# A small input loaded as 16 rows of 36 elements and spread by four accumulating matmuls, in place of 64 rows of nine and one

## The chip, the cores and the metric

One core of a Trainium2 chip. The metric is the device time of one execution, in microseconds (us). Every run here counts as fast unless it lies over 1.5% above the fastest of its kernel.

## The reference

Two attention layers with one query each, side by side. A looks at the last 2,048 of 8,192 cached keys and values (W = min(4096, max(256, 8192/4))), B at all of them. Cut to what matters:

```python
D, Hq, Hkv, Sk, Dh = 576, 32, 16, 8192, 128        # x: [1, 1, 576], bf16
q = (x @ wq).reshape(B, Sq, Hq, Dh)                # wq: [576, 4096]
scores = einsum(q, k) * Dh ** -0.5                 # two query heads per cached head
o = softmax(scores) @ v
out = o.reshape(B, Sq, Hq * Dh) @ wo               # wo: [4096, 576]; A and B concatenated
```

x has 1,152 bytes for each layer. The caches that are read and the weights have 102.76 MB.

## The kernel before

A helper records every operation with what it reads and writes, and works out the waits. The engines are SP (issues the large loads), ACT, DVE, POOL and PE. For the projection the kernel wants, in each of 128 partitions, nine values of x: partition p holds part p // 2, and odd and even partitions use different halves of them. x is loaded as 64 rows of nine, and a matmul with a matrix `twice`, an identity with each column doubled, copies row p // 2 to partition p:

```python
    xnine = nc.alloc_sbuf_tensor("xnine", [64, 2, 9], BF16)
    twice = nc.alloc_sbuf_tensor("twice", [64, 128], BF16)
    # ... cut
    def load_x(P):                                     # issued from ACT, P = 0 for A, 1 for B
        def go(act):
            return act.dma_start(xnine[:, P, :], xs[P][0, 0, :].rearrange("(m r) -> m r", m=64))
        add("act", go, writes=[("xnine", P)], dma="x%d" % P)
    # ... cut: POOL clears tiles, then makes the identity
    add("dve", lambda dve: dve.tensor_copy(twice[:, :].rearrange("p (m e) -> p m e", e=2), <identity, each column twice>),
        reads=["ident"], writes=["twice"])
    add("pe", lambda pe: pe.matmul(misc[:, 320:338], lhsT=twice[:, :], rhs=xnine[:, :, :].rearrange("p a r -> p (a r)"),
                                   start=True, stop=True),
        reads=[("xnine", 0), ("xnine", 1), "twice"], writes=[B_M])
```

What follows, in order:

```python
    WQ = [(4 * SLOT - WQ_W, [("v", 2)]), (SLOT, [("k", 1, 0), ("k", 1, 1), ("v", 0)])]
    for P in range(2):
        off, res = WQ[P]
        x_columns(P)                       # DVE: four masked copies of the spread x
        load(slots[:, off:off + WQ_W], <wq of P>, res, "wq%d" % P)      # SP, 4,608 KB
        q_part(P, off, res)                # PE: 36 matmuls of 512 columns, the projection
        q_finish(P)                        # ACT copy, PE turns, DVE copy
    # ... cut
    for g in range(NG):                    # group 0 is A, groups 1 to 4 are B
        for s in range(2):
            load_k(g, s)                   # SP; s = 1 reuses the place of wq of B
        load_v(g)                          # SP; reuses the place of wq of A
        # ... cut: transposes, scores, softmax, weighted sum
```

All large loads are issued from SP in one order. And the second half of K of A (`load_k(0, 1)`) is put where wq of B lies, so SP waits for the second projection before it issues that load, and every load behind it waits too.

## Time and profile before

| | before |
|---|---|
| time, median of 3 runs | 245.37 us (245.37 to 245.59) |
| profiled span | 244.0 us |
| bytes read | 102.76 MB, 421 GB/s over the span |
| PE, ACT, DVE, POOL busy | 68%, 38%, 36%, 3% |
| x of B lands | 17.8 us |
| first, second projection start | 18.82, 24.80 us |
| second half of K of A is issued | 28.24 us |

How to read it: the lines are shown in the prediction below. In a timeline the columns are start, duration, engine, source line, operation, tiles, count, and in brackets how long the engine had idled and what ended it. "PEld" is the load of a matmul's weights, "SPq" the queue of loads issued from SP. An engine's idle time matters only if it stands on the chain that ends last; here the row of the transfer engines, busy in all slices but the last, is the first thing to look at. A group of instructions is cut at the edge of the window that was asked for: the line of the first projection in the prediction (x32, 3.60 us) ends at 22 us; whole, it is x36 and 4.03 us. The trace also has a record of every DMA packet: its start, length and bytes. Figures said to come from the packet records are from there.

### The profile page before, as it was taken

What the parts mean: (1) busy time and instruction counts of PE and PEld (TensorE: products, weight loads), DVE (VectorE), ACT (ScalarE), POOL (GpSimd) and SP (SyncE); (2) the same over time, 40 slices, a digit from 0 to 9 for tenths busy, and PEclk for the clock granted to TensorE, in tenths of its full rate; (3) what the DMA queues carried; (4) which work ended last, traced back from release to release, by engine and by line L of the source; (5) the groups of instructions that cost most, each with busy time, mean ns of one, the idle gap of its engine ahead of it and who ended that gap; (6) DMA issues with size and microseconds to landing.
All of it is one profiled execution on the core that took longest, in us unless ns stands there. A gap on an engine that the chain in (4) does not pass through costs nothing. (4 is left out here: it accounts for less than half of the span.)

```text
span 244.0 us, 5212 instructions
## 1 busy us (share of the span) xinstructions
PE 165.8 (68%) x2325; PEld 120.5 (49%) x2325; DVE 88.2 (36%) x152; ACT 93.2 (38%) x96; POOL 6.4 (3%) x33
## 2 busy tenths in 40 slices
PE   0007539958397997394999473999446699845964
PEld 0002238745237775243978231987332687535753
DVE  0001218855304555203465322456322165533030
ACT  2000018845303876301687500678600387630000
POOL 5000100000000000000000000000000000000000
PEclk9999959997867999657699959799958799965799
DMA  9999999999999999899999999999989999989994
GB/s 344 429 405 422 435 432 422 427 424 427 459 432 426 489 397 462 371 430 435 483 410 451 403 403 435 435 494 408 473 365 440 430 494 397 473 380 417 426 405 172
DMA packets 4064, 102.88 MB, mean 422 GB/s; under 512 B 596, under 2 KB 728, under 8 KB 984
## 3 DMA queue, kind: packets, MB, share of 16 engines
q1 hardware_dynamic: 3896, 102.76, 98.3%
q8 instruction: 6, 0.10, 0.2%
q10 hardware_dynamic: 160, 0.00, 0.0%
q14 instruction: 2, 0.02, 0.0%
HBM read 102.76 MB, written 0.00 MB: 421 GB/s over the span
## 5 line engine op out<-in xcount | busy, mean ns | idle before, releaser
L506 ACT ACTIVATE kt<-ktps 128x1024 bf16<-128x1024 bf16 x80 | 79.8, 1040 | 87.3 <-PE ktps L496 87.2
L496 PE MATMUL ktps<-ident,slots 128*128 128x128 bf16 x1280 | 87.9, 234 | 22.6 <-PEq L214 19.6
L496 PEld LDWEIGHTS ktps<-ident,slots 128*128 128x128 bf16 x1280 | 81.7, 106 | 38.5 <-issue 38.5
L509 DVE COPY kt<-ktps 128x1024 bf16<-128x1024 bf16 x80 | 60.7, 774 | 59.6 <-PE ktps L496 59.6
L588 PE MATMUL opsum<-slots,ptm 128*32 128x512 bf16 x320 | 27.4, 515 | 7.7 <-PEq L214 7.7
L521 PE MATMUL sacc<-kt,qst 128*32 128x512 bf16 x320 | 25.8, 398 | 2.3 <-PEq L214 2.3
L588 PEld LDWEIGHTS opsum<-slots,ptm 128*32 128x32 bf16 x320 | 13.3, 125 | 20.3 <-issue 18.0
L559 PE MATMUL misc<-ident,psb 128*128 128x128 bf16 x40 | 4.3, 271 | 15.8 <-PEq L214 15.8
L547 ACT ACTIVATE psb<-sacc,stat 128x2048 bf16<-128x2048 f32 x5 | 9.8, 1967 | 9.8 <-DVE stat L536 9.8
L606 DVE TENSOR_TENSOR vtmp<-opsum,maskV 128x512 f32<-128x512 f32 x4 | 2.8, 691 | 27.7 <-PE opsum L588 27.7
L438 PE MATMUL misc<-xnine,twice 64*128 64x18 bf16 x1 | 0.2, 170 | 17.8 <-DMA xnine<-in_B_x_dram 17.8
L559 PEld LDWEIGHTS misc<-ident,psb 128*128 128x128 bf16 x40 | 3.1, 118 | 18.3 <-issue 18.3
L521 PEld LDWEIGHTS sacc<-kt,qst 128*32 128x32 bf16 x320 | 5.0, 94 | 8.4 <-issue 4.9
L566 DVE TENSOR_TENSOR ptm<-misc,maskP 128x1024 bf16<-128x1024 bf16 x5 | 3.5, 692 | 15.6 <-PE misc L559 15.6
L438 PEld LDWEIGHTS misc<-xnine,twice 64*128 64x128 bf16 x1 | 0.1, 99 | 17.8 <-issue 17.8
L703 ACT ACTIVATE outsb<-ktps 64x144 bf16<-64x144 f32 x1 | 0.3, 288 | 21.1 <-PE ktps L691 21.1
L691 PE MATMUL ktps<-slots,opj 128*32 128x144 bf16 (+1 forms) x192 | 6.8, 247 | 2.2 <-DMA slots<-in_B_wo_dram 2.2
L462 ACT ACTIVATE qrow<-opsum 128x512 bf16<-128x512 f32 x1 | 0.6, 597 | 19.2 <-PE opsum L456 19.2
L691 PEld LDWEIGHTS ktps<-slots,opj 128*32 128x32 bf16 x192 | 5.2, 97 | 3.6 <-DMA slots<-in_B_wo_dram 3.0
L447 DVE TENSOR_SCALAR xpad<-misc,par 128x5 bf16<-128x5 f32 (+1 forms) x8 | 1.2, 228 | 13.6 <-PE misc L438 13.6
L481 POOL COPY qst<-qcol 128x32 bf16<-128x32 bf16 x8 | 1.7, 213 | 147.5 <-PE sacc L521 147.5
L559 PE MATMUL turned<-ident,psb 128*128 128x128 bf16 x40 | 5.3, 314 | 0.0
(76 smaller groups left out, 57.9 us busy)
## 6 DMA issues: line engine op xcount, KB each, us to landing
slots<-in_B_k_cache_dram SPq DMA_DIRECT2D x8, 4096.0 KB
slots<-in_A_k_cache_dram SPq DMA_DIRECT2D x4, 2048.0 KB
slots<-in_A_v_cache_dram SPq DMA_DIRECT2D x4, 2048.0 KB
slots<-in_A_wq_dram SPq DMA_DIRECT2D x1, 4608.0 KB, 13.9
slots<-in_B_wq_dram SPq DMA_DIRECT2D x1, 4608.0 KB, 24.0
slots<-in_A_wo_dram SPq DMA_DIRECT2D x1, 4608.0 KB, 19.8
slots<-in_B_wo_dram SPq DMA_DIRECT2D x1, 3024.0 KB, 26.6
slots<-in_B_wo_dram SPq DMA_DIRECT2D x1, 1008.0 KB, 9.2
```

The costliest lines, as they stand in the source:

```text
L447: add("dve", lambda dve, dst=dst, o=320 + 9 * P + i, n=n, e=e: dve.tensor_scalar(dst, misc[:, o:o + n], par2[:, e:e + 1], None, ALU.mult), ...
L481: return pool.tensor_copy(dst, src)
L496: ins = pe.matmul(ktps_bf[q][:, t * 128:(t + 1) * 128], lhsT=slots[:, o:o + 128], rhs=ident[:, :], start=True, stop=True, is_transpose=True)
L506: add("act", lambda act, src=src, dst=dst: act.activation(dst, src, ACT.Copy), reads=[("bank", q)], writes=[("kt", u % NKT, q)], tag="e%d% ...
L509: add("dve", lambda dve, src=src, dst=dst: dve.tensor_copy(dst, src), reads=[("bank", q)], writes=[("kt", u % NKT, q)], tag="e%d%d" % (u, q))
L521: ins = pe.matmul(sacc[32 * j:32 * j + 32, :], lhsT=qst[:, o:o + 32], rhs=rhs, start=(u == 0 and e == 0), stop=True, skip_group_check=True)
L547: return act.activation(dst, src, ACT.Exp, bias=st(C_NB + g), scale=SCALE, accum_out=st(C_L + g))
L559: ins = pe.matmul(dst[:, t * 128:(t + 1) * 128], lhsT=psb[:, o:o + 128], rhs=ident[:, :], start=True, stop=True, is_transpose=True)
L566: return dve.tensor_tensor(ptm[:, c * 1024:(c + 1) * 1024].rearrange("p (t y) -> p t y", t=8), dst.rearrange("p (t y) -> p t y", t=8), mas ...
L588: ins = pe.matmul(opsum[64 * j + 32 * x:64 * j + 32 * x + 32, :], lhsT=ptm[:, o:o + 32], rhs=v[:, at[0], at[1], :, :, b:b + 128], start=(n ...
L606: add("dve", lambda dve: dve.tensor_tensor(vtmp[:, :, :], src, by, ALU.mult), reads=[B_O, w], writes=["vtmp"], tag="keep")
L691: ins = pe.matmul(ktps[P + j // 2][32 * j:32 * j + 32, 0:w], lhsT=opj[:, P, at:at + 32], rhs=slots[:, o:o + w], start=(jj == 0), stop=(jj ...
```

## The change

The intent: rows of nine elements are pieces of 18 bytes, 64 for each x. With 16 rows of 36 elements there are a quarter as many pieces, of 72 bytes. Row k then holds parts 4k to 4k + 3, so partition p needs columns 9c to 9c + 8 of row p // 8, with c = (p // 2) mod 4. Four matmuls, one for each c, each with a selection matrix that is zero outside its partitions, add up to the same result in the same place.

```diff
-    xnine = nc.alloc_sbuf_tensor("xnine", [64, 2, 9], BF16)
-    twice = nc.alloc_sbuf_tensor("twice", [64, 128], BF16)
+    xnine = nc.alloc_sbuf_tensor("xnine", [16, 2, 36], BF16)
+    twice = nc.alloc_sbuf_tensor("twice", [16, 4, 128], BF16)
...
-                return act.dma_start(xnine[:, P, :], xs[P][0, 0, :].rearrange("(m r) -> m r", m=64))
+                return act.dma_start(xnine[:, P, :], xs[P][0, 0, :].rearrange("(m r) -> m r", m=16))
...
-        for t in (ident, xpad, selq, warm, identf, pick, pickB, qst):
+        for t in (ident, twice, xpad, selq, warm, identf, pick, pickB, qst):
             pool.memset(t[:], 0.0)
...  (the set-up's list of writes gains "twice0")
-    add("dve", lambda dve: dve.tensor_copy(twice[:, :].rearrange("p (m e) -> p m e", e=2),
-                                           bass.AP(tensor=ident, offset=0, ap=[[128, 64], [1, 64], [0, 2]])),
-        reads=["ident"], writes=["twice"])
-    add("pe", lambda pe: pe.matmul(misc[:, 320:338], lhsT=twice[:, :], rhs=xnine[:, :, :].rearrange("p a r -> p (a r)"),
-                                   start=True, stop=True),
-        reads=[("xnine", 0), ("xnine", 1), "twice"], writes=[B_M])
+    add("dve", lambda dve: dve.tensor_copy(bass.AP(tensor=twice, offset=0, ap=[[512, 16], [130, 4], [8, 16], [1, 2]]),
+                                           bass.AP(tensor=ident, offset=0, ap=[[128, 16], [0, 4], [1, 16], [0, 2]])),
+        reads=["ident", "twice0"], writes=["twice"])
+
+    def x_spread(pe):
+        for c in range(4):
+            ins = pe.matmul(misc[:, 320:338], lhsT=twice[:, c, :], rhs=xnine[:, :, 9 * c:9 * c + 9],
+                            start=(c == 0), stop=(c == 3))
+        return ins
+    add("pe", x_spread, reads=[("xnine", 0), ("xnine", 1), "twice"], writes=[B_M])
```

More of the change, by code (lines that the diff above doesn't have):

```diff
@@ L377, in setup @@
         return pool.memset(opj[:], 0.0)
-    add("pool", setup, writes=["ident", ("xpad", 0), ("xpad", 1), "selq", "ones", "warm", "identf", "pick", "pickB",
+    add("pool", setup, writes=["ident", "twice0", ("xpad", 0), ("xpad", 1), "selq", "ones", "warm", "identf", "pick", "pickB",
                                ("qst", 0), ("qst", 1), ("opj", 0), ("opj", 1)])
```

## The prediction

> **What bounds the kernel now.** I read the page first: the slices, the DMA queues, the chain that ended last. Then the timeline of the first 32 us, where all the changed code runs, the DMA queue's own waits, and the trace's records of single DMA packets.
>
> The slices (a tenth is the busy share of 6.1 us) and the queues:
>
> ```profile
> DMA  9999999999999999899999999999989999989994
> GB/s 344 429 405 422 435 432 422 427 424 427 459 432 426 489 397 462 371 430 435 483 410 451 403 403 435 435 494 408 473 365 440 430 494 397 473 380 417 426 405 172
> q1 hardware_dynamic: 3896, 102.76, 98.3%
> q10 hardware_dynamic: 160, 0.00, 0.0%
> ```
>
> The reader is to see that the transfer engines are busy from the first slice to the last but one. All large loads are on q1, in one order of issue; q10 holds the two loads of x, 160 packets of next to no time. Busiest engine beside them: the PE at 68%. The kernel is one stream of 102.76 MB, so the time is the stream's length, its start-up, and a tail.
>
> The chain of waits, at its end:
>
> ```profile
> 231.52 0.33 SPq L398
> 231.85 0.04 issue
> 231.89 9.93 DMA slots<-in_B_wo_dram
> 241.82 0.04 issue
> 241.87 0.64 PE ktps L691 x16
> ```
>
> A load of 144 KB takes 9.93 us because it stands behind the rest of the queue. The chain starts at 216 us; neither x nor anything made from it is in it.
>
> The timeline where x is used (start, duration, engine, instruction, then the idle time before it and what ended that):
>
> ```profile
> 0.80 0.55 ACTq L366 DMA_DIRECT2D xnine<-in_A_x_dram  x1
> 1.37 0.61 ACTq L366 DMA_DIRECT2D xnine<-in_B_x_dram  x1
> 4.24 0.26 DVE L435 COPY twice<-ident 64x128 bf16<-64x128 bf16 x1
> 17.84 0.17 PE L438 MATMUL misc<-xnine,twice 64*128 64x18 bf16 x1 [17.84 <-DMA xnine<-in_B_x_dram]
> 18.05 0.62 DVE L447 TENSOR_SCALAR xpad<-misc,par 128x5 bf16<-128x5 f32 x4 [13.55 <-PE misc L438]
> 18.82 3.60 PE L456 MATMUL opsum<-slots,xpad 128*32 128x512 bf16 x32 [0.81 <-DVE xpad L447]
> 23.96 0.61 DVE L447 TENSOR_SCALAR xpad<-misc,par 128x5 bf16<-128x5 f32 x4
> 24.80 3.40 PE L456 MATMUL turned<-slots,xpad 128*32 128x512 bf16 x36 [0.99 <-DMA slots<-in_B_wq_dram]
> 28.24 1.20 SPq L411 DMA_DIRECT2D slots<-in_A_k_cache_dram  x2
> 34.67 5.31 PE L496 MATMUL ktps<-ident,slots 128*128 128x128 bf16 x64 [5.52 <-PEq L214]
> ```
>
> The last landing of x (17.8 us) does hold up the first projection: its weights, wq of A, are issued at 0 and take 13.9 us to land, so 18.82 - 13.9 = 4.9 us are lost there. But the second projection starts at 24.80, when wq of B lands, and its x columns are ready at 23.96 + 0.61 = 24.57. The loss on A is absorbed before B, by 0.23 us.
>
> Who makes the stream wait, from the DMA queue's own waits:
>
> ```profile
> SPq L411 <- PE turned L456: 25.7, 1, 25.7
> ```
>
> That is the only wait of the early loads: the second half of K of A waits for the second projection and goes out at 28.24. By then the first half (2 x 2,048 KB, queued since 1.2) is still streaming; its transposes start at 34.67. Allowing the 1.05 us from issue to first packet that the first load shows in the packet records, the queue has 34.67 - 28.24 - 1.05 = about 5.4 us in hand. No stream time depends on x unless x becomes later by more than that.
>
> **What the Trainium skill says.** (1) "DMA: Bandwidth & Descriptors", section "Queues, rings and completion order": each DMA engine takes turns between its queues, a packet at a time. The trace agrees: a packet of x waits for one of wq, 36,864 B and 1.364 us, before each of its own. Section "Why a DMA increments its semaphore by 16 and not by 1" says that the engine count is the largest up to 16 that divides the slowest dimension of both sides, and that each engine adds a semaphore write. That gives 64 rows = 4 packets plus 1 on each of 16 engines, for two loads 2 x 5 x 16 = 160, which is q10's count. (2) Same page, section "Specifications": below 512 B an engine does read-modify-write. One would fear dear packets of 18 B. The records say otherwise: each lasts 9 ns, and wq's packets follow one another every 1.366 us with one of x between, every 1.360 us without: 6 ns each. (3) "TensorE: Matmul & The Clock Gate", section "Part 1: The HAM clock gate": the PE is at half rate after about 3.4 us of idleness. Both projections start that way (four 512-column matmuls side by side come every 0.43 us in both), after whatever idle time, so a longer pause before the second changes little.
>
> **The change part by part.**
>
> *The loads.* 64 rows of 18 B become 16 rows of 72 B: 1 packet plus 1 semaphore write on each engine for each load, 2 x 2 x 16 = 64 packets in place of 160. Six fewer for each engine at 6 to 9 ns: 0.036 to 0.054 us of stream, say 0.05 us. This is the only part that lies on the path that sets the end.
>
> *When x lands.* In the records the first round of x's packets starts between 5.3 and 6.4 us, each further round 1.366 us later; the last of x of B goes at 17.35 and lands 0.4 us after. After the change there are four rounds: 6.4 + 3 x 1.366 + 0.4 = about 10.9 us for the last, in place of 17.8. (Two rounds may share a turn, as some do now, then 9.5.)
>
> *The selection.* One matmul of 0.17 us becomes four accumulating ones of the same 18 columns. The four small matmuls that turn a q row take 0.27 us together in this trace, so about 0.27 us: +0.10 us, on a PE that idles from 0 to 17.8.
>
> *The selection matrix.* The copy into `twice` writes 128 elements in each of 16 rows in place of 64; rows run side by side, so 0.26 us as now. New is a memset of 512 bf16 on POOL, second in the set-up; the one of 576 bf16 takes 0.58 us, so 0.58 x 512/576 = 0.52 us. All behind it moves by that: the identity from 4.0 to about 4.5, `twice` from 4.50 to about 5.0. Still 5.9 us before x lands.
>
> *What starts earlier.* x columns of A: 10.9 + 0.27 + 0.7 = 11.9 us. The first projection then waits for its weights, and starts at 13.9 in place of 18.82. It ends about 4.9 us sooner (22.89 - 4.9 = 18.0), and the x columns of B are ready at 24.57 - 4.9 = 19.7. The second projection still starts when wq of B lands, at 24.8 minus those 0.05 us; K of A's second half is still issued at 28.2.
>
> *Sum.* +0.10 us on the PE and +0.52 us on POOL, both hidden by over 5 us; -4.9 us on the first projection, hidden by the wait for wq of B; -0.05 us on the stream. 245.37 - 0.05 = 245.3 us.
>
> **The rivals.** *The wait for x is real: the 4.9 us reach the end.* For it: the largest PE idle time of the start, 17.84 us, is put down to x. Against it: the second projection names wq of B as its releaser, and the stream shows no hole. It would give 245.4 - 4.9 = 240.5 us, just on the line of 2%. I give it 2 in 100.
>
> *Small packets cost more than their records show*, through writes below 512 B in the memory or the engine. For it: GB/s of the slices from 6 to 18 us swing between 405 and 429, a little under the 435 at 24. Against it: the 6 ns measured between large packets leave no room, and the records of those packets, 36,864 B in 1.364 us, are as long with x between as without. At ten times the cost it would be -0.4 us: 245.0 us.
>
> *A later set-up or a colder PE bites.* The memset moves the identity, and the PE now pauses some 5 us before the second projection in place of about 1 us. Were the second projection wholly at half rate, it would last 3.9 us, as the first (36 x 0.107), and not 3.4: K of A's second half would be issued 0.5 us later, out of 5.4 us in hand. Time 245.3 us. Only if the queue ran dry would it cost 0.5 us.
>
> *Something unrelated moves*: addresses after the two resized tiles, the phase of the clock gate over the PE's 2,300 matmuls, the order of landings in the tail. The times before span 0.22 us; I allow about 0.5 us to both sides.
>
> **Range and chances.** The middle is 245.3. Down to 244.8 covers dear small packets and a lucky tail; up to 245.8 a late reissue or an unlucky tail. Two per cent is 4.9 us: faster needs the first rival in full, slower a hole in the stream of which no part of the change shows a source. Faster 0.015, within 2% 0.975, slower 0.01.
>
> **What would show it.** In the profile after: q10 with 64 packets; x of B landing near 11 us; four selection matmuls at about 11 us, the first projection at about 13.9 with wq of A as its releaser; the second at 24.7 to 24.8 with wq of B still as its releaser; K of A's second half issued at 28 to 28.8; its transposes' start near 34.6; DMA tenths as before; the same end of the chain. Wrong if wq of A or B lands more than 0.3 us sooner (small packets were dear), if x still lands after 13.9 (rounds misread), if the queue shows a hole before 40 us, or if the second projection starts before 24.5.

## More of the kernel before

The experiments ran on two chips: the first eight on one, the last four (128 early matmuls, 128 between the projections, 512 pieces of 72 B, and 2,048 pieces together) on another; each is compared with the kernel before of its own job (245.47 to 245.57 us on the first, 245.48 us on the second).

Of the kernel before, 34 runs were made in this study; they lie between 245.22 and 245.99 us.

## The result, and the profile after

The changed kernel takes 245.37 us (median of 6 runs, 245.18 to 245.63), the kernel before 245.38 us (6 runs, 245.25 to 245.59). The ratio is 1.0, with a 95% interval of 0.9987 to 1.0012. A ratio here is the mean time of one kernel's fast runs over that of the other's of the same rounds, so it is not quite the ratio of the medians quoted beside it. The profiled run took 245.18 us; its span is 243.8 us.

The page of the changed kernel, slices and queue of the small loads, against the same rows in the prediction:

```profile
DMA  9999999999999999899999999999989999989994
GB/s 351 424 442 403 430 433 422 430 425 427 449 427 433 485 398 462 371 435 430 485 409 452 419 403 435 435 489 398 473 366 430 435 489 419 462 374 423 422 406 175
...
q10 hardware_dynamic: 64, 0.00, 0.0%
```

The row of tenths is the same digit for digit. The queue of x has 64 packets, as forecast from 16 rows over 16 engines, in place of 160.

The changed kernel's timeline of the same stretch:

```profile
0.94 0.52 POOL L375 MEMSET twice<- 16x512 bf16 x1
...
4.69 0.25 DVE L435 COPY twice<-ident 16x128 bf16<-16x128 bf16 x1
...
11.01 0.25 PE L441 MATMUL misc<-xnine,twice 16*128 16x18 bf16 x4 [11.01 <-DMA xnine<-in_B_x_dram]
11.30 0.63 DVE L451 TENSOR_SCALAR xpad<-misc,par 128x5 bf16<-128x5 f32 x4 [6.35 <-PE misc L441]
...
13.89 4.03 PE L460 MATMUL opsum<-slots,xpad 128*32 128x512 bf16 x36 [2.64 <-DMA slots<-in_A_wq_dram]
...
24.78 4.03 PE L460 MATMUL turned<-slots,xpad 128*32 128x512 bf16 x36 [5.88 <-DMA slots<-in_B_wq_dram]
...
28.86 1.20 SPq L411 DMA_DIRECT2D slots<-in_A_k_cache_dram  x2
...
34.67 1.54 PE L500 MATMUL ktps<-ident,slots 128*128 128x128 bf16 x13 [4.90 <-PEq L214]
```

Read it from top to bottom. x of B is there at 11.0 us, 6.8 us sooner. The first projection moves from 18.82 to 13.89, and its releaser is now wq of A, no longer x. The second starts at 24.78, 0.02 us sooner, and the idle time before it has grown from 0.99 to 5.88 us: this is where the 4.9 us went. The transposes of K start at 34.67 in both.

One thing is later. The second projection took 4.03 us and not 3.40, so the second half of K of A went out at 28.86 and not at 28.24. The clock records show why: the full PE clock was granted from 27.41 us in the profile of before, from 29.37 us in this one.

The chain that ended last, changed kernel:

```profile
232.82 0.33 SPq L398
233.15 0.04 issue
233.19 8.42 DMA slots<-in_B_wo_dram
241.61 0.04 issue
241.65 0.64 PE ktps L695 x16
```

It is the same chain: a small last load behind the rest of the queue, then the output matmuls. The last load landed at 241.82 before and at 241.61 here.

### The profile page after: what moved, and what is told of

The parts are those of the page before. It is cut to its first block, busy times and chain, and to the rows that moved or that the text cites. A ratio compares the mean times of both kernels' runs of the same rounds, so it can differ in the third digit from the quotient of the medians.

```text
span 243.8 us, 5219 instructions
## 1 busy us (share of the span) xinstructions
PE 164.0 (67%) x2328; PEld 119.3 (49%) x2328; DVE 88.2 (36%) x152; ACT 93.2 (38%) x96; POOL 6.8 (3%) x34
## 5 line engine op out<-in xcount | busy, mean ns | idle before, releaser
L500 PE MATMUL ktps<-ident,slots 128*128 128x128 bf16 x1280 | 86.0, 231 | 19.9 <-PEq L214 17.4
L500 PEld LDWEIGHTS ktps<-ident,slots 128*128 128x128 bf16 x1280 | 79.8, 104 | 35.5 <-issue 35.4
L460 PE MATMUL turned<-slots,xpad 128*32 128x512 bf16 x36 | 4.0, 630 | 5.9 <-DMA slots<-in_B_wq_dram 5.9
L475 DVE CAST qcol<-misc 128x32 bf16<-128x32 f32 x2 | 0.6, 300 | 17.2 <-PE misc L471 17.2
L460 PE MATMUL opsum<-slots,xpad 128*32 128x512 bf16 x36 | 4.0, 630 | 2.6 <-DMA slots<-in_A_wq_dram 2.6
```

The lines of the kernel that those rows point to most:

```text
L460: ins = pe.matmul((turned if P else opsum)[32 * j:32 * j + 32, :], lhsT=xpad[:, P, u, :], rhs=slots[:, o:o + 512], start=(u == 0), stop=(u ...
L500: ins = pe.matmul(ktps_bf[q][:, t * 128:(t + 1) * 128], lhsT=slots[:, o:o + 128], rhs=ident[:, :], start=True, stop=True, is_transpose=True)
```

## The experiments

Theory: the time is the length of the one stream of large loads. The change moves an event that the stream does not depend on, until the second half of K of A would go out too late to keep the queue filled. Rivals: the wait for x was on the path, or lies hidden whatever happens; two real effects cancel; a small packet costs far more than its record; the PE or the issue of K sets the end.

### The added work alone

The kernel before with the selection tile of four slices, its memset and four matmuls, while x stays 64 rows of nine. (The change's other half cannot be run by itself: one matmul cannot spread rows of 36.)

```diff
-    twice = nc.alloc_sbuf_tensor("twice", [64, 128], BF16)
+    twice = nc.alloc_sbuf_tensor("twice", [64, 4, 128], BF16)      # slices 1 to 3 stay zero
+        for t in (ident, twice, xpad, ...
+        for c in range(4):
+            ins = pe.matmul(misc[:, 320:338], lhsT=twice[:, c, :], rhs=<all of xnine>, start=(c == 0), stop=(c == 3))
```

> The kernel before, with the added work alone: selection tile of 64 x 4 x 128 (slices 1 to 3 zero), its memset first in line on POOL, four accumulating selection matmuls; x still comes as 64 rows of nine. My theory (the time is the length of the load stream, and all of this is hidden): 245.4 us within 0.3; q10 with 160 packets, x of B landing at 17.8, four matmuls of about 0.25 us together, first projection at about 18.9, second at 24.8 released by wq of B, second half of K of A issued between 28.2 and 28.9. Rival (the added work costs something that the smaller x load pays back, so that the equal times are two effects cancelling): 246.0 us or more.

Measured: 245.45 us (4 runs, 245.31 to 245.76), before 245.57 us, ratio 1.0001 (0.9985 to 1.0018). Its timeline:

```profile
17.81 0.25 PE L440 MATMUL misc<-xnine,twice 64*128 64x18 bf16 x4 [17.81 <-DMA xnine<-in_B_x_dram]
...
18.87 4.03 PE L459 MATMUL opsum<-slots,xpad 128*32 128x512 bf16 x36 [0.81 <-DVE xpad L450]
...
24.77 2.13 PE L459 MATMUL turned<-slots,xpad 128*32 128x512 bf16 x36 [0.91 <-DVE xpad L450]
...
26.94 1.20 SPq L411 DMA_DIRECT2D slots<-in_A_k_cache_dram  x2
```

The added work costs nothing that shows, so no two effects of more than about 0.4 us, the width of the interval, cancel. One thing was not as expected: the first matmul of the second projection names the x columns of B (ready at 24.63 us) as its releaser, its weight load at 24.74 us names wq of B. The two came 0.1 us apart. The run gave more than asked. The full clock came at 23.06 us, the second projection took 2.13 us, and K went out at 26.94, earlier than the expected 28.2 to 28.9; still the profiled run took 245.41 us. With x as late as before, the second projection was the fastest of the three. The pause in front of it does not decide its length: 0.91 us here and 0.99 us before went with 2.13 and 3.40 us. The times at which the full clock was granted (23.06, 27.41 and, after the change, 29.37 us) stand in the same order as the lengths.

### x later, by 14 us and by 24 us

In the changed kernel the two loads of x are issued from SP, behind wq of B in one run and behind the first half of K of A in the other. Loads go out in the order in which they are recorded, so the edit moves lines:

```diff
-    load_x(0); load_x(1)                 # from ACT, first of all
+    for P in range(2): load(<wq of P>)   # from SP
+    load_k(0, 0)                         # only in the second run
+    load_x(0); load_x(1)                 # from SP
```

> The changed kernel with x made late: its two loads queued on SP behind wq of B. My theory (x costs nothing until the second half of K of A is issued after about 33.4 us, because the stream has 5 us in hand): x of B lands at about 25.0, 14 us later than in the changed kernel; first projection 26 to 30, second about 31.8 to 33.8 if warm or 35.8 if cold; K issued between 33.9 and 35.9, its first packets 1.05 us later, against a queue that runs dry at about 34.5: a hole of 0.5 to 2.5 us, time 245.9 to 247.9 us. Rival 1 (the wait for x lies on the path as it stands): 245.4 + 14 = 259 us. Rival 2 (x is hidden anyway, whenever it comes): 245.4 us.

> The same with x queued behind the first half of K of A. My theory: x of B lands at about 34.7; first projection 35.7 to 39.7, second 41.5 to 43.5 or 45.5; K issued between 43.6 and 45.6, first packets at 44.7 to 46.7 against a queue dry at about 34.5: a hole of 10.2 to 12.2 us which nothing later can make good, since the stream never pauses again: 255.6 to 257.6 us. Rival 1 (x on the path one for one): 245.4 + 23.7 = 269 us. Rival 3 (the stream has slack later that makes good part of the hole): 250 us or so, with lower DMA share before but higher GB/s after.

Measured: 247.75 us (4 runs: 246.87, 249.85, 247.99, 247.50) and 258.10 us (4 runs: 257.06, 259.10, 258.86, 257.33); before 245.57 us. Ratios 1.0121 (1.0075 to 1.0166) and 1.0527 (1.0492 to 1.0563). The timeline of the first of the two runs:

```profile
24.97 0.25 PE L447 MATMUL misc<-xnine,twice 16*128 16x18 bf16 x4 [24.97 <-DMA xnine<-in_B_x_dram]
...
33.45 1.20 SPq L409 DMA_DIRECT2D slots<-in_A_k_cache_dram  x2
```

And three windows of the second (the last two columns are the share of the transfer engines and their GB/s):

```profile
33.00:34.00 1.00, 0.00 (x0) 0.00 (x0) 0.00 (x0) 0.00 (x0) 0.00 (x0) 1.00 0.20 68
34.00:45.00 11.00, 7.17 (x91) 3.32 (x92) 1.72 (x11) 1.19 (x2) 1.07 (x8) 1.00 0.00 0
45.00:46.00 1.00, 1.00 (x22) 1.00 (x20) 0.93 (x5) 0.72 (x1) 0.00 (x0) 1.00 1.08 328
```

Here is the hole that the theory asks for: no byte moves for 11 us, while the late projections run and K waits for them. The packet records put the hole from 33.58 to 34.84 us in the first run and from 33.53 to 45.08 us in the second (fewer than half of the engines busy), 1.3 and 11.5 us. Both profiled runs are longer than the changed kernel's by nearly that: 246.87 and 257.06 against 245.18 us, 1.7 and 11.9 us. Nothing is made good later. Of 14 us and 24 us of lateness, only what reached past the queue's end counted, so the wait for x is neither on the path one for one (259 and 269 us) nor hidden for good (245.4 us).

The expected ranges were too low at their upper ends: 249.85 us against 247.9, 259.10 against 257.6; of the second run the median too, 258.10 us, lies outside. The hole shows the reason for a part. The queue is dry at 33.5 us, not 34.5, and half of the engines have a packet 1.40 us after the issue (the first packet comes after 1.31 and 1.33 us), not 1.05. So, with 33.55 between the two, K must go out by 33.55 - 1.40 = 32.15 us, which leaves the kernel before an estimated 32.15 - 28.24 = 3.9 us in hand. The unprofiled runs may have had slower projections as well; they left no trace.

### A longer stream

The changed kernel with one load of 2 MiB more between wq of A and wq of B, into the tile for transposed keys, which is free then. A small matmul makes the PE wait for it.

```diff
+        if P == 0:
+            load(kt[:, 0:2, :], <2 MiB of a key cache>, [("kt", u, q) for u in range(2) for q in range(4)], "more")
```

> The changed kernel with 2 MiB more in the stream: one load into the tile for transposed keys, which is free until 35 us, queued between wq of A and wq of B. My theory (the time is the bytes over some 427 GB/s, from 102.76 MB in the 240.7 us between the first packet and the last): 2.097 MB / 427 GB/s = 4.9 us more, 250.3 us within 0.5; wq of B lands at about 29.7 and everything after moves by as much. Rival (the end is set by the PE or by waits between loads, and the stream has room): 246 us or less.

Measured: 250.36 us (4 runs, 250.25 to 250.42), before 245.47 us: 4.9 us more, as worked out, ratio 1.0196 (1.0182 to 1.0211). Its timeline:

```profile
29.61 4.03 PE L460 MATMUL turned<-slots,xpad 128*32 128x512 bf16 x36 [10.15 <-DMA slots<-in_B_wq_dram]
...
33.69 1.20 SPq L411 DMA_DIRECT2D slots<-in_A_k_cache_dram  x2
```

Bytes in the stream cost their full time. K goes out at 33.69 us here, later than in the first run with a hole, and the packet records show no hole: the queue before it is longer by the same 4.9 us. It also shows why the 4.9 us that the first projection gained were worth nothing: they were not bytes.

### The price of a small packet

The change saves six packets on each engine. To see what one costs, the changed kernel got one more load behind x on ACT's queue, into a scratch tile that nothing reads, in three forms.

```diff
+    small = nc.alloc_sbuf_tensor("small", [64, 32, 9], BF16)       # 2,048 pieces of 18 B, 64 B apart in memory
+    act.dma_start(small[:, :, :], <wq, 64 rows, 32 pieces of 9 of each>)
+    # second form: [64, 8, 36], 512 pieces of 72 B
+    # third form:  [64, 32, 16][:, :, 0:9], 2,048 pieces of 18 B, next to one another in memory
```

> The changed kernel with one more load behind x on ACT's queue: 2,048 pieces of 18 B into a scratch tile that nothing reads, 128 packets and a semaphore write more on each of the 16 engines, interleaved with the large loads. My theory (a small packet takes 6 to 9 ns of an engine's time, wherever it stands): 129 x 6 to 9 ns = 0.8 to 1.2 us more, 246.2 to 246.6 us; the packets of 36,864 B follow one another every 1.366 us while the small ones run between them. Rival (small packets are dear, 66 ns each, and the six fewer of the change saved 0.4 us that something else took back): 129 x 66 = 8.5 us more, 254 us.

> As the run with 2,048 pieces of 18 B, which took 2.8 us more, but the same bytes in 512 pieces of 72 B, the ratio of the change itself. If the cost goes by the packet (2.8 us over 129 packets an engine, 22 ns each): 33 x 22 ns = 0.7 us, 246.2 us within 0.3. If it goes by the bytes or by the mere presence of a second queue: 248 us again. If it goes by the 9 to 12 ns of a packet's own record alone: 0.3 to 0.4 us, 245.8 us.

> As the run with 2,048 pieces of 18 B, but each row's 32 pieces lie next to one another in memory, as x does, and are spread only in the scratch tile; in the first form they lay 64 B apart. If the 22 ns of a small packet come from the packet: 248.2 us again. If they came from the scattered reads, and a packet of x costs only the 6 ns seen between wq's packets: 129 x 6 to 9 ns, 246.2 to 246.6 us.

| pieces | packets more on each engine | time | before, same job | difference | for each packet |
|---|---|---|---|---|---|
| 2,048 of 18 B, apart | 129 | 248.24 us | 245.47 us | 2.77 us | 21 ns |
| 512 of 72 B | 33 | 246.03 us | 245.48 us | 0.55 us | 17 ns |
| 2,048 of 18 B, together | 129 | 248.03 us | 245.48 us | 2.55 us | 20 ns |

The page of the first form:

```profile
q10 hardware_dynamic: 2128, 0.04, 0.5%
```

The bytes are the same in all three, so the cost goes with the number of packets, not with the bytes, and how the pieces lie in memory matters little (2.77 against 2.55 us). On average it is 17 to 21 ns, not the 6 to 9 that were expected of these loads and not the 66 of the rival. The packet records show where a part of the rest is: a small packet's own record is 9 ns in the first form, but the large ones beside it got longer (those of 16,384 B, between 38 and 60 us, from 616 to 622 ns; between 26 and 33 us from 611 to 624), and where they overlapped by 3 ns they stood 4 ns apart. What makes them longer no run tells. The price is not even along the way either. Set against the packet records of the changed kernel, the two forms with 129 packets are 0.9 and 1.3 us late when 11 MB have moved (at 28 to 29 us, after 18 of their packets on each engine), the form with 33 packets 0.3 us. From there to 50 MB, over 108 packets more, they lose another 1.7 and 1.4 us: 13 to 16 ns each. So 17 to 21 ns is the mean over a whole load, and what the early loss is stays open.

For x itself the reading of the prediction stands as it was made: beside x, the packets of 36,864 B last 1.364 us in both kernels with a small packet between and without, and follow one another 6 ns later with one than without. wq of B releases the second projection 0.02 us sooner after the change. By that reading the six packets are worth about 0.04 us, by the mean of these loads 0.10 to 0.13 us, both estimates; the runs of either kernel scatter over more than that.

### K earlier, and a surprise

To move the issue of K alone, idle matmuls between the two projections were to keep the PE at its full clock. Their output is overwritten.

```diff
+        if P == 0:
+            for i in range(80):           # 128 in the last run of the study
+                pe.matmul(turned[32 * j:32 * j + 32, :], lhsT=xpad[:, 0, 0, :], rhs=<512 columns of wq>, start=True, stop=True)
```

> The changed kernel with 80 idle matmuls between the projections, which keep the PE busy until wq of B lands (their output is overwritten; the result stays right). My theory: the second projection runs at the full rate, 36 x 0.054 = about 2 us in place of 4.03, so the second half of K of A is issued at about 26.9 in place of 28.9, and nothing comes of it: 245.4 us within 0.3. Rival (the issue of K, which waits 26 us for the second projection, is on the path): 243.4 us.

Measured: 247.19 us (4 runs: 246.66, 248.54, 247.56, 246.81), before 245.57 us, ratio 1.0088 (1.0055 to 1.0120). Neither 245.4 nor 243.4. The second projection took 2.13 us, but K went out at 27.80 us and not at the expected 26.9, because wq of B released that projection only at 25.63 us. The packet records show a fetch of instructions, one packet of 16,384 B, at 23.48 us. Of the later runs, two more have such a fetch ahead of that point (80 and 128 tiny matmuls, at 23.73 and 10.00 us), and wq of B releases the projection at 25.89 and 25.57 us there; in the kernel before, the changed kernel and the run with 16 idle matmuls, which have none so early, at 24.60 to 24.80 us. The delay cost nothing at the end of those two traces (245.4 and 245.7 us). (The run with 128 wide matmuls has such a fetch too, at 23.57 us, but its PE is busy until 27.8 us.)

The last load landed at 241.83, as in the kernel before (241.82). The loss in the profiled run comes after it, in the chain's last steps:

```profile
233.33 8.50 DMA slots<-in_B_wo_dram
241.83 0.04 issue
241.88 0.61 PE ktps L695 x15
242.49 1.01 issue
243.50 0.25 PE ktps L695
```

The sixteenth of the last output matmuls started 1.01 us after the fifteenth had ended, with nothing to wait for that the profile shows. The packet records have a fetch of instructions, 16,384 B, on their own queue from 241.08 to 242.18 us, which ends 0.3 us before the wait begins. The edit had put 160 PE instructions (80 matmuls and 80 weight loads) in front, and so moved the places where fetches fall. The Trainium skill, "Runtime: NRT & Kernel Launch", section "Instruction fetch mechanics", says that instructions come in blocks of 16 KiB, 256 instructions each, fetched by DMA, and that crossing a block is mostly hidden. That gives a test: 160 more instructions move the blocks against the tail, 256 do not. The trace agrees as to the size: each such fetch is one packet of 16,384 B, and there are six of them in the changed kernel and seven in either run with 256 instructions more. Four more runs vary this.

> As the run with 80 idle matmuls between the projections, but with 16 of four times the array work: 32 PE instructions more in place of 160. In that run the second half of K of A went out at 27.8 in place of 28.9 and the last load ended at 241.8 as before, but the PE then waited 1.01 us for nothing that the profile shows, with an instruction fetch of 16 KB begun at 241.1. My theory (the 1.8 us came from 160 more instructions to fetch, not from the clock or the earlier load): 245.4 us within 0.4, K issued at about 26.9. Rival (an earlier issue of K, or a PE that is warm at 25 us, costs time itself): 247 us again.

> The changed kernel with 80 tiny matmuls (32 weights, 8 columns) where the PE idles, between 4.5 us and the landing of x: 160 PE instructions more and nothing else changed in the part where the projections run. My theory (the number of instructions ahead of the tail moves the fetch of the last ones into the tail): 246.7 to 248.5 us as in the run with 80 idle matmuls between the projections, with a PE wait of about 1 us near the end that no engine or load explains. Rival (it was the earlier K, or the warm PE): 245.4 us within 0.3.

> As the run with 80 tiny early matmuls, but with 128: 256 PE instructions more in place of 160. Some runs of the 80 took 246.6 and 248.4 us, others 245.2, where 17 runs of the kernel before lay between 245.2 and 246.0. [...]Theory (the place of the cuts against the tail makes the slow runs): all runs within 245.1 to 246.0. Rival (more instructions ahead, wherever they are cut, make slow runs): some runs over 246.5, as with 80.

> As the run with 80 idle matmuls between the projections, which took 246.7 to 248.5 us, but with 128 of them: 256 PE instructions more in place of 160, and more PE work. They end later than wq of B lands, at some 27 to 28 us, so the second half of K of A is issued at 29.5 to 31.5, still ahead of the 32.15 us that the late-x run gives as the last moment (queue dry at 33.55, 1.40 us from issue to first packet). If the cut of the instruction fetches against the tail made that run slow: 245.4 us within 0.4. If a busy PE between the projections, or the sheer number of instructions, made it slow: 247 us or more.

The edits: 16 idle matmuls of full width between the projections (first), and 80 or 128 tiny ones ahead of x_spread, where the PE idles:

```diff
+        for _ in range(80):               # or 128
+            pe.matmul(misc[0:32, 400:408], lhsT=ident[:, 0:32], rhs=ident[:, 0:8], start=True, stop=True)
```

| PE instructions more | where | runs, us | median |
|---|---|---|---|
| 160 (80 wide) | between the projections | 246.66 to 248.54 (4) | 247.19 |
| 160 (80 tiny) | before x | 245.37, 245.46, 248.36, 246.56, 245.16, 245.68 | 245.57 |
| 32 (16 wide) | between the projections | 245.28 to 246.21 (6) | 245.46 |
| 256 (128 tiny) | before x | 245.28 to 245.69 (5) | 245.48 |
| 256 (128 wide) | between the projections | 245.22 to 245.59 (6) | 245.42 |

The 16 idle matmuls missed their aim. They ran at the full clock, were done by 22.2 us, and the second projection ran slow again (3.81 us), so this run says nothing on an early K. That an early K does not cost time the run with the added work alone shows (26.94 us, 245.4 us). The 80 tiny ones missed their forecast as well: expected at 246.7 to 248.5 us, their median is 245.57. With 256 more, in either place, all eleven runs lie where those of the kernel before do: there neither a PE that is busy right through nor the number of instructions costs time. With 160 more, four of four and two of six are slow (over 246.5 us).

That fits the cut of the fetches, and so do the packet records: in the last ten microseconds the changed kernel and both runs with 256 have two fetches, begun at 237.4 to 238.6 and at 241.0 to 242.1 us, the two runs with 160 only one (241.08 and 239.91 us). It is not shown. All runs with 160 were made on one chip and all with 256 on another, so the chip is a rival that no run excludes, though the kernel before is equally fast on both. The traced run of the 80 tiny ones has the moved cut and is fast, so the cut alone is not enough. Only one slow run has a trace; its 1.01 us are most of what it lies above the kernel before (246.66 against 245.57 us), but less than the 1.6 us between the medians.

For the theory these runs have another use. The timeline of the run with 128 wide ones:

```profile
18.80 9.17 PE L725 MATMUL turned<-slots,xpad 128*32 128x512 bf16 x128
...
27.80 2.11 PE L460 MATMUL turned<-slots,xpad 128*32 128x512 bf16 x36
...
29.97 1.20 SPq L411 DMA_DIRECT2D slots<-in_A_k_cache_dram  x2
```

The second projection started 3.0 us late here. Put in order, K went out at 26.94 (added work alone), 28.24 (before), 28.86 (after), 29.97 (128 wide) and 33.45 us (x behind wq), and the profiled runs took 245.4, 245.4, 245.2, 245.2 and 246.9 us. Flat up to 29.97, risen at 33.45: the queue's reserve, seen as a curve. The 32.15 in between is worked out; no run was made there. The run with 80 idle matmuls (27.80 us, 246.7 us) is left out, as its loss lies in the tail.

## Why the prediction was right or wrong

Right as to the time (245.3 forecast, 245.37 measured) and as to its reason. That nothing changes is an easy forecast, and many reasons would give it; what tests this one is its steps and the runs in which the same reason had to give 4.9 and 11.9 us. By its steps:

- *One stream sets the time.* Shown: 2 MiB more cost 4.9 us, as worked out; a hole of 11.5 us cost 11.9 us.
- *x lands at about 10.9 us.* 11.0. The reading by rounds, each small packet behind one large one, held: 64 packets, four rounds.
- *The four selection matmuls 0.27 us, the memset 0.52 us, the copy 0.26 us, all hidden.* 0.25, 0.52 and 0.25 us; the run with them alone shows no cost.
- *The first projection gains 4.9 us, which the wait for wq of B swallows.* It started 4.93 us sooner, and the idle time before the second grew by 4.89 us.
- *K's second half at 28.2, or up to 28.8 us.* 28.86. That a longer pause "changes little" was too mild: the second projection took 4.03 us and not 3.40. It was wholly at the slow clock, the case that the third rival allowed for, and it cost nothing.
- *About 5.4 us in hand.* Too much: 3.9 us. The prediction took the start of the transposes, 34.67, for the end of the queue's work. The last packets are over at 33.5; landing and release come about a microsecond later. And it took the 1.05 us from issue to first packet of the very first load, where the load into the emptied queue took 1.31 to 1.33 us to its first packet and 1.40 us until half of the engines had one. The conclusion stood, because the change used only 0.6 us of it.
- *6 to 9 ns for a small packet, 0.05 us in all.* Open. The spacing of the packets of wq gives 6 ns for one of x in both kernels. It does not hold for small packets at large: in loads of 33 and 129 of them on each engine the mean was 17 to 21 ns, and the large packets themselves became longer, which that reading could not show. The term is too small to be seen in the time either way, and the change's own saving was not measured apart.
- *"Neither x nor anything made from it" in the chain that ended last.* Loosely read: the scores in that chain come from the projections, and so from x. What the chain does not hold is a wait for x.

The rivals: the wait for x on the path is refuted by the result; dear small packets (66 ns) by the three loads of small pieces; two cancelling effects by the run of the added work alone.

## What to carry to other kernels

The longest wait of an engine is worth nothing if the next step waits for something else anyway: follow the event to what it releases in the resource that is busy all the time, and work out how late it may come. Measure that reserve at the last packet, not at the consumer's start, and with the issue latency of a queue found empty. And when an experiment adds instructions, check with a second count of them (here 256 in place of 160), and on the same chip, that their number alone does not move the time.

## What the Trainium skill lacked or had wrong

- "DMA: Bandwidth & Descriptors", section "Specifications", gives a first-byte latency of about 0.6 us for loads issued from SP or ACT. Here the first load's first packet came 1.04 us after its issue, that of a load into an emptied queue 1.31 to 1.33 us, and that of x, on the second queue beside large loads, 3.9 us (changed kernel) to 4.5 us (before).
- The same page, section "Bandwidth", has about 10.5 ns per packet as the floor of small transfers, measured on loads issued from GpSimd. Here, with loads issued from ACT beside a stream of large packets, a small packet cost 17 to 21 ns of each engine's time on average, for 18 B and 72 B alike. The section does not say that the large packets beside it become longer, as they did here (616 to 622 ns for those of 16,384 B).
- "Runtime: NRT & Kernel Launch", section "Instruction fetch mechanics", calls crossing a 16 KiB block mostly hidden. With all transfer engines busy, one PE wait of 1.01 us came 0.3 us after such a fetch at the end of the kernel; that the fetch caused it is not shown. Runs with 160 instructions more were up to 3.2 us slower than the changed kernel's median (248.54 against 245.37), runs with 256 more, on another chip, were not. The section does not speak of fetches that stand beside a kernel's own loads: in three runs with one ahead of wq of B its landing let the second projection start at 25.57 to 25.89 us, in three without at 24.60 to 24.80 us.
